# Strassen's seven products in the second dense layer of a fused attention and feed-forward kernel

## The chip, the cores and the metric

The kernel runs on one core of one Trainium2 chip. The metric is the device time of one execution in microseconds (us), the median of several; one execution is taken with the hardware profiler, and its views are what is called "the profile" or "the trace" here. Most times of one kernel agree within about 0.3%.

## The reference

For 8 batches and 12 heads of 448 tokens, attention without softmax, then a two-layer feed-forward on the 3584 tokens:

```python
scores = scale * q @ k.T                      # head_dim 64
attn   = maximum(scores, 0) ** 2 / S
x      = (attn @ v), heads side by side       # 3584 x 768
h      = x @ w_in                             # 768 x 2048
g      = h * sigmoid(1.702 * h)
out    = g @ w_out                            # 2048 x 768, float32
```

## The kernel before

Tokens are worked on in 8 groups of 3 or 4 tiles of 128 (3,4,3,4,3,4,3,4). While the first layer of group g runs on TensorE, the second layer of group g-1 is mixed in, and every 4.8 us of modelled dense time an attention "visit" (three score steps, sometimes one attention-value step) is put between. I call "stage g" the time from the first first-layer matmul of group g to that of group g+1, and "tail" what follows the last first-layer matmul. A "piece" is a run of matmuls that add up in one bank of PSUM, the memory that TensorE writes to. The bank is free for the next piece when another engine has read it out; for the second layer I call that the eviction. All dense pieces, whichever layer, share a pool of two PSUM banks:

```python
ps_s = ctx.enter_context(tc.tile_pool(name="ps_s", bufs=3, space=bass.MemoryType.PSUM))  # 2 banks each
ps_m = ctx.enter_context(tc.tile_pool(name="ps_m", bufs=2, space=bass.MemoryType.PSUM))  # 1 bank each
...
def release():                       # the third score step of a visit is held until now
    while held:
        u, j, sc = held.pop()
        ats[u, j] = relu2(u, j, sc)  # relu on ScalarE, square (at) on VectorE
...
def m1(g, f):                        # first layer, 6 matmuls of 384 or 512 columns
    ht = ps_m.tile([128, 512], F32, name="ht", tag="mm")
    ...                              # gelu on ScalarE empties the bank, GpSimd scales into gt
    release()

def m2(g, m, h):                     # second layer, 16 matmuls of 384 columns
    op = ps_m.tile([128, 512], F32, name="op", tag="mm")
    for f in range(NF):
        nc.tensor.matmul(out=op[:, 0:w], lhsT=gts[g][:, f, m * 128:(m + 1) * 128], rhs=..., ...)
    nc.vector.tensor_scalar(out=ot[:, lo:lo + w], in0=op[:, 0:w], ...)   # eviction on VectorE
    ...
    release()
```

After a visit the inputs of a later unit are prepared: k is cast to float16 on VectorE, q on GpSimd, and both are transposed by DMA.

## Time and profile before

| | before |
|---|---|
| median (lowest to highest) | 403.76 us (403.63 to 404.41), 3 runs |
| span of the profiled run | 402.6 us |
| TensorE / VectorE / ScalarE / GpSimd busy | 95 / 47 / 51 / 33% |
| second-layer matmuls | 912 |
| waits of TensorE after 110 us | none listed |

The page's chain line follows the work that ended last back to the start, and gives each engine's share of the span:

```profile
PE 87%; DVE 5%; ACT 4%; issue 2%; DMA 1%; POOL 0%; ACTq 0%; POOLq 0%
```

TensorE is the bound; the others appear on the chain only in the first quarter. The further lines stand in the prediction.

### The profile page before, as it was taken

The page shows a single profiled execution, that of the slowest core. Times are in us where ns is not written, and L with a number is a line of the kernel's source. Part 1 is how long each engine was busy: PE and PEld are TensorE (multiplying, and loading weights), DVE is VectorE, ACT ScalarE, POOL GpSimd, SP SyncE. Part 2 cuts the span into 40 slices and gives each one's busy share as a digit, 9 for nine tenths or more (in the row PEclk, how much of TensorE's full clock was granted, in tenths as well). Part 3 has the DMA queues.
Part 4 walks back from the last instruction along what each step waited for, and adds up shares of the span by engine and source line. Part 5 has one row for each costly group of instructions (what it writes and reads, how often), then busy time and mean ns, then how long its engine had stood idle before and what let it go on. Part 6 is the DMA issues. An engine that isn't in the chain of part 4 may idle for free.

```text
span 402.6 us, 7803 instructions
## 1 busy us (share of the span) xinstructions
PE 384.2 (95%) x3200; PEld 202.9 (50%) x3200; DVE 187.7 (47%) x296; ACT 204.8 (51%) x295; POOL 133.7 (33%) x200
## 2 busy tenths in 40 slices
PE   7678999999999999999999999999999999999995
PEld 3343545344455555445455555445455555555564
DVE  2886674267655554546446555556444311010121
ACT  3885671576764554665555546566646411322100
POOL 8454425442533223424324232313311222323100
PEclk9989999999999999999999999999999999999999
DMA  8999998988688666573786189915400111111133
GB/s 122 192 205 205 204 277 194 276 147 176 159 181 178 158 126 157 150 145 82 178 157 130 11 192 198 189 22 77 86 16 26 39 41 40 41 39 41 39 80 79
DMA packets 65220, 50.85 MB, mean 126 GB/s; under 512 B 35744, under 2 KB 61728, under 8 KB 65184
## 3 DMA queue, kind: packets, MB, share of 16 engines
q1 hardware_dynamic: 47792, 35.60, 37.2%
q0 software_dynamic: 17152, 14.55, 24.3%
q8 instruction: 25, 0.41, 0.4%
q10 hardware_dynamic: 240, 0.20, 0.2%
q14 instruction: 11, 0.09, 0.1%
HBM read 45.61 MB, written 11.01 MB: 141 GB/s over the span
## 4 chain that ended last, share of the span: by engine, by line
PE 87%; DVE 5%; ACT 4%; issue 2%; DMA 1%; POOL 0%; ACTq 0%; POOLq 0%
PE op L304 36%; PE ht L275 35%; PE sc L141 8%; PE av L166 7%; ACT rl L155 4%; DVE at L156 2%; DMA q<-in_q_dram 1%; DVE qT L131 1%; PE tr L127 1%; DVE rl L152 1%; ACT gf L280 1%; DVE xt L183 0%; DVE kT L131 0%; DVE k L102 0%; POOL k L117 0%
## 5 line engine op out<-in xcount | busy, mean ns | idle before, releaser
L155 ACT ACTIVATE rl<-sc 128x896 f16<-128x896 f32 x165 | 146.0, 920 | 71.7 <-PE sc L141 71.6
L275 PE MATMUL ht<-xt,win 128*128 128x384 f16 (+1 forms) x768 | 157.2, 353 | 1.4 <-DVE xt L183 1.0
L304 PE MATMUL op<-wout,gt 128*128 128x384 f16 (+1 forms) x912 | 153.2, 323 | 0.0
L282 POOL TENSOR_SCALAR gt<-gf 128x384 f16<-128x384 f32 (+1 forms) x128 | 80.1, 626 | 216.5 <-ACT gf L280 215.9
L156 DVE TENSOR_TENSOR at<-rl 128x896 f16<-128x896 f16 x168 | 110.9, 664 | 85.0 <-ACT rl L155 84.7
L280 ACT ACTIVATE gf<-ht 128x384 f32<-128x384 f32 (+1 forms) x128 | 70.3, 549 | 98.4 <-PE ht L275 86.1
L304 PEld LDWEIGHTS <-gt 128*128 128x128 f16 x912 | 88.3, 98 | 60.1 <-issue 1.6
L275 PEld LDWEIGHTS <-win 128*128 128x128 f16 x768 | 71.3, 98 | 77.6 <-issue 16.7
L310 DVE TENSOR_SCALAR osb<-op 128x384 f32<-128x384 f32 (+1 forms) x57 | 31.4, 550 | 115.2 <-PE op L304 115.2
L141 PE MATMUL sc<-qT,kT 64*64 64x448 f16 x672 | 49.3, 366 | 8.7 <-DVE qT L131 3.6
L166 PE MATMUL av<-at,v 64*64 64x448 f16 x672 | 37.8, 359 | 2.0 <-DVE at L156 1.6
L141 PEld LDWEIGHTS <-kT 64*64 64x64 f16 x672 | 18.3, 107 | 35.2 <-issue 22.7
L183 DVE CAST xt<-av 128x768 f16<-128x768 f32 (+2 forms) x36 | 26.8, 772 | 2.5 <-PE av L166 2.5
L166 PEld LDWEIGHTS <-v 64*64 64x64 f16 x672 | 20.2, 109 | 14.3 <-issue 3.9
L89 POOL DMA_DIRECT2D v<-in_v_dram x24 | 17.9, 748 | 16.7 <-PE sc L141 11.0
L102 POOL CAST q<-qst 128x896 f16<-128x896 f32 x18 | 17.3, 964 | 0.2
L102 DVE CAST k<-kst 128x896 f16<-128x896 f32 x18 | 14.8, 821 | 0.0
L131 DVE COPY kT<-tr 128x896 f16<-128x896 f16 x6 | 3.7, 621 | 6.9 <-PE tr L127 6.9
L322 POOL DMA_DIRECT2D win<-in_moe_w_in_dram x8 | 5.4, 682 | 2.3 <-DMA q<-in_q_dram 1.2
L117 POOL DMA_DIRECT2D q<-in_q_dram x6 | 4.3, 719 | 4.1 <-PE sc L141 2.4
L117 POOL DMA_DIRECT2D k<-in_k_dram x6 | 4.5, 757 | 2.2 <-DMA v<-in_v_dram 1.4
L358 PE MATMUL zp<-zero 128*128 128x512 f16 x8 | 3.6, 628 | 1.2 <-DVE zero L355 1.2
(18 smaller groups left out, 27.5 us busy)
## 6 DMA issues: line engine op xcount, KB each, us to landing
out_dram<-osb SPq DMA_DIRECT2D x54, 192.0 KB, 2.7
kst<-in_k_dram SPq DMA_DIRECT2D x18, 448.0 KB, 5.2
qst<-in_q_dram SPq DMA_DIRECT2D x18, 448.0 KB, 5.7
v<-in_v_dram POOLq DMA_DIRECT2D x24, 224.0 KB, 5.1
win<-in_moe_w_in_dram POOLq DMA_DIRECT2D x8, 384.0 KB, 11.5
wout<-in_moe_w_out_dram POOLq DMA_DIRECT2D x4, 768.0 KB, 11.4
k<-in_k_dram POOLq DMA_DIRECT2D x6, 224.0 KB, 9.0
q<-in_q_dram POOLq DMA_DIRECT2D x6, 224.0 KB, 8.8
```

What stands on the lines that cost most here:

```text
L89: nc.gpsimd.dma_start(out=x, in_=quad(v, b, pr))
L102: eng.tensor_copy(out=o, in_=i)
L141: nc.tensor.matmul(out=sc[c, a, 0:S], lhsT=st["kT"][r, j, c], rhs=st["qT"][r, :, c], start=True, stop=True)
L155: nc.scalar.activation(out=rl, in_=sc[:, :, 0:S], func=AF.Relu)
L156: nc.vector.tensor_tensor(out=at, in0=rl, in1=rl, op=ALU.mult)
L166: nc.tensor.matmul(out=st["av"][64 * a:64 * a + 64, s, 0:S], lhsT=st["v16"][r, a, 64 * j:64 * j + 64], rhs=at[r, a, :], start=(j == 0), st ...
L183: nc.vector.tensor_copy(out=xts[g][:, 2 * pr:2 * pr + 2, 64 * (lo - gcum[g]):64 * (hi - gcum[g])], in_=av[:, :, 64 * (lo - b * J):64 * (hi ...
L275: nc.tensor.matmul(out=ht[:, 0:n], lhsT=w[:, kk, fo:fo + 128], rhs=xts[g][:, kk, 0:n], start=(kk == 0), stop=(kk == NK - 1))
L280: nc.scalar.activation(out=gf[:, 0:n], in_=ht[:, 0:n], func=AF.Gelu_apprx_sigmoid, scale=1.0 / SC)
L282: nc.gpsimd.tensor_scalar(out=gts[g][:, f, 0:n], in0=gf[:, 0:n], scalar1=SC, scalar2=1.0, op0=ALU.mult, op1=ALU.mult)
L304: nc.tensor.matmul(out=op[:, 0:w], lhsT=gts[g][:, f, m * 128:(m + 1) * 128], rhs=wout[h][f // WO][:, f % WO, part * w:(part + 1) * w], sta ...
L310: nc.vector.tensor_scalar(out=ot[:, lo:lo + w], in0=op[:, 0:w], scalar1=1.0 / SC, scalar2=None, op0=ALU.mult)
```

## The change

From group 1 on, pairs of tiles are multiplied by Strassen's scheme (halves of d_ff and halves of the output columns): seven products of 8 matmuls instead of eight. To pay for it, sums of activation halves are formed on VectorE, sums of weight halves once on VectorE and GpSimd, and the products are combined in the evictions (ScalarE for the first two, VectorE for the rest) with three additions per pair on GpSimd. An odd tile is done with the same weights at its old matmul count. Some buffers shrink to make room. The core of the diff:

```diff
-    stp = ctx.enter_context(tc.tile_pool(name="stp", bufs=3))
+    stp = ctx.enter_context(tc.tile_pool(name="stp", bufs=2))
-    osp = ctx.enter_context(tc.tile_pool(name="osp", bufs=4))
+    osp = ctx.enter_context(tc.tile_pool(name="osp", bufs=3))
...
+    def pair(g, m, n):
+        A = [[part_of(g, m + i, j) for j in range(2)] for i in range(2)]
+        if n == 0:
+            asum(5, None, A[0][0], A[0][1], ALU.add)
...
+        elif n == 3:
+            asum(1, None, A[0][0], A[1][1], ALU.add)
+        elif n == 4:
+            asum(6, A[1][0], A[1][0], A[0][0], ALU.subtract)
...
+        op = bank()
+        if n == 0:
+            product(A[0][0], w_b, op)
+            evac(ea, op, None)                       # ScalarE
...
+        elif n == 3:
+            product(sums[2], wout[0][0], op)
+            evac(o1[:, lo], op, eb)                  # VectorE
+            nc.gpsimd.tensor_tensor(out=eb, in0=ec, in1=o1[:, lo], op=ALU.subtract)
+        elif n == 4:
+            product(sums[7], w_e, op)
+            evac(o0[:, lo], op, ea)
+        elif n == 5:
+            product(sums[1], w_a, op)
+            evac(o0[:, lo], op, o0[:, lo])
+            evac(o1[:, hi], op, eb)
...
+            c = [("single", g - 1, nm - 1, h) for h in (1, 0)] if nm % 2 else []
+            c += [("pair", g - 1, m, n) for m in range(0, nm - 1, 2) for n in range(7)]
...
+                weight_sum(w_e, wout[0][1], wout[1][1], ALU.add, i, nc.vector)
+                if i == gblk[0] // 2 - 1:
+                    weight_sum(w_e, wout[0][1], wout[1][1], ALU.add, 3, nc.vector)
+                    for i in range(4):
+                        weight_sum(w_d, wout[1][0], wout[0][0], ALU.add, i, nc.gpsimd)
```

More of the change, by code (lines that the diff above doesn't have):

```diff
@@ L55 @@
     gfp = ctx.enter_context(tc.tile_pool(name="gfp", bufs=3))
-    gtp = ctx.enter_context(tc.tile_pool(name="gtp", bufs=2))
-    osp = ctx.enter_context(tc.tile_pool(name="osp", bufs=4))
+    gtp = ctx.enter_context(tc.tile_pool(name="gtp", bufs=1))
+    smp = ctx.enter_context(tc.tile_pool(name="smp", bufs=1))
+    osp = ctx.enter_context(tc.tile_pool(name="osp", bufs=3))
     ps_s = ctx.enter_context(tc.tile_pool(name="ps_s", bufs=3, space=bass.MemoryType.PSUM))
@@ L63 @@
     warm = cst.tile([1, 1], F32, name="warm")
-    zero = cst.tile([128, 512], F16, name="zero")
     win = [cst.tile([128, NK, WQ * 128], F16, name=f"win{i}") for i in range(NF // WQ)]
@@ L67 @@
             for h in range(2)]
+    wsum = [cst.tile([128, WO, NOUT], F16, name=f"wsum{i}") for i in range(3)]
     units = {}
@@ L269, in m1 @@
         if f == 0:
-            gts[g] = gtp.tile([128, NF, 512], F16, name="gt", tag="gt")
+            gts[g] = gtp.tile([128, NF, n], F16, name="gt", tag=f"gt{g % 2}")
         ht = ps_m.tile([128, 512], F32, name="ht", tag="mm")
@@ L298, in m2 @@
         ot = osb[g, m]
-        last = g == NG - 1 and m == gblk[g] // 2 - 1
-        for part in range(2 if last and h == 1 else 1):
-            w = NOUT // 2 if last and h == 1 else NOUT
-            op = ps_m.tile([128, 512], F32, name="op", tag="mm")
-            for f in range(NF):
-                nc.tensor.matmul(
-                    out=op[:, 0:w],
-                    lhsT=gts[g][:, f, m * 128:(m + 1) * 128],
-                    rhs=wout[h][f // WO][:, f % WO, part * w:(part + 1) * w],
-                    start=(f == 0), stop=(f == NF - 1))
-            lo = h * NOUT + part * w
-            nc.vector.tensor_scalar(out=ot[:, lo:lo + w], in0=op[:, 0:w],
-                                    scalar1=1.0 / SC, scalar2=None, op0=ALU.mult)
-            if last:
-                store(g, m, lo, lo + w, (nc.sync, nc.scalar))
@@ L314, in m2 @@
-        if h == 1 and not last:
+        op = ps_m.tile([128, 512], F32, name="op", tag="mm")
+        for f in range(NF):
+            nc.tensor.matmul(
+                out=op[:, 0:NOUT],
+                lhsT=gts[g][:, f, m * 128:(m + 1) * 128],
+                rhs=wout[h][f // WO][:, f % WO, :],
+                start=(f == 0), stop=(f == NF - 1))
+        lo = h * NOUT
+        nc.vector.tensor_scalar(out=ot[:, lo:lo + NOUT], in0=op[:, 0:NOUT],
+                                scalar1=1.0 / SC, scalar2=None, op0=ALU.mult)
@@ new lines, in m2, with weight_sum, part_of, asum @@
+        if h == 1:
+            store(g, m, 0, DM, (nc.sync, nc.sync))
+        release()
+    HF = NF // 2
+    w_a, w_b, w_c = wsum
+    w_d, w_e = wout[1][0], wout[0][1]
+    def weight_sum(o, x, y, op, i, eng):
+        c = slice(2 * i, 2 * i + 2)
+        eng.tensor_tensor(out=o[:, c, :], in0=x[:, c, :], in1=y[:, c, :], op=op)
+    def part_of(g, m, i):
+        return gts[g][:, i * HF:(i + 1) * HF, m * 128:(m + 1) * 128]
+    sums = {}
+    def asum(n, out_, x, y, op):
+        if out_ is None:
+            out_ = smp.tile([128, HF, 128], F16, name=f"as{n}", tag=f"as{n}")
+        nc.vector.tensor_tensor(out=out_, in0=x, in1=y, op=op)
+        sums[n] = out_
@@ new lines, in product, with bank, evac @@
+    def product(lhs, w, op, start=True, stop=True, c0=0, cw=NOUT):
+        for f in range(HF):
+            nc.tensor.matmul(
+                out=op[:, 0:cw], lhsT=lhs[:, f, :], rhs=w[:, f, c0:c0 + cw],
+                start=(start and f == 0), stop=(stop and f == HF - 1))
+    def bank():
+        return ps_m.tile([128, 512], F32, name="op", tag="mm")
+    def evac(o, op, add, w=NOUT):
+        if add is None:
+            nc.scalar.activation(out=o, in_=op[:, 0:w], func=AF.Copy, scale=1.0 / SC)
+        else:
+            nc.vector.scalar_tensor_tensor(out=o, in0=op[:, 0:w], scalar=1.0 / SC, in1=add,
+                                           op0=ALU.mult, op1=ALU.add)
@@ new lines @@
+    et = {}
+    def pair(g, m, n):
+        A = [[part_of(g, m + i, j) for j in range(2)] for i in range(2)]
+        last = g == NG - 1 and m == gblk[g] // 2 - 2
+        if n == 0:
+            asum(5, None, A[0][0], A[0][1], ALU.add)
+            for x in "ab":
+                et[x] = smp.tile([128, NOUT], F32, name=f"e{x}", tag=f"e{x}")
+            for i in range(2):
+                osb[g, m + i] = osp.tile([128, DM], F32, name="osb", tag="osb")
+        elif n == 1:
+            asum(2, None, A[1][0], A[1][1], ALU.add)
+        elif n == 2:
+            asum(7, A[0][1], A[0][1], A[1][1], ALU.subtract)
+        elif n == 3:
+            asum(1, None, A[0][0], A[1][1], ALU.add)
+        elif n == 4:
+            asum(6, A[1][0], A[1][0], A[0][0], ALU.subtract)
+        lo, hi = slice(0, NOUT), slice(NOUT, DM)
+        o0, o1 = osb[g, m], osb[g, m + 1]
+        ea, eb, ec = et["a"], et["b"], o1[:, hi]
+        if n == 6 and last:
+            w = NOUT // 2
+            for p in range(2):
+                op = bank()
+                product(sums[6], w_d, op, c0=p * w, cw=w)
+                c = slice(NOUT + p * w, NOUT + (p + 1) * w)
+                evac(o1[:, c], op, o1[:, c], w)
+                store(g, m + 1, c.start, c.stop, (nc.sync, nc.scalar))
+            return
+        op = bank()
+        if n == 0:
+            product(A[0][0], w_b, op)
+            evac(ea, op, None)
+        elif n == 1:
+            product(A[1][1], w_c, op)
+            evac(eb, op, None)
+            nc.gpsimd.tensor_tensor(out=ec, in0=ea, in1=eb, op=ALU.add)
+        elif n == 2:
+            product(sums[5], wout[1][1], op)
+            evac(o0[:, hi], op, ea)
+            nc.gpsimd.tensor_tensor(out=ea, in0=ec, in1=o0[:, hi], op=ALU.subtract)
+        elif n == 3:
[9 more added lines that the diff above has]
+            evac(o1[:, hi], op, eb)
+            store(g, m, 0, DM, (nc.sync, nc.sync))
+            if last:
+                store(g, m + 1, 0, NOUT, (nc.sync, nc.sync))
+        else:
+            product(sums[6], w_d, op)
+            evac(o1[:, hi], op, o1[:, hi])
+            store(g, m + 1, 0, DM, (nc.sync, nc.sync))
+        release()
@@ new lines, in single @@
+    def single(g, m, h):
+        A = [part_of(g, m, j) for j in range(2)]
+        if h == 1:
+            osb[g, m] = osp.tile([128, DM], F32, name="osb", tag="osb")
+            asum(3, None, A[0], A[1], ALU.add)
+        op = bank()
+        product(A[1 - h], (w_c, w_b)[h], op, stop=False)
+        product(sums[3], wout[h][h], op, start=False)
+        nc.vector.tensor_scalar(out=osb[g, m][:, h * NOUT:(h + 1) * NOUT], in0=op[:, 0:NOUT],
+                                scalar1=1.0 / SC, scalar2=None, op0=ALU.mult)
+        if h == 0:
@@ L353 @@
         nc.scalar.activation(out=warm, in_=warm, func=AF.Gelu_apprx_sigmoid)
-        nc.vector.memset(zero, 0.0)
+        zero = gfp.tile([128, 1024], F16, name="zero", tag="gf")
+        nc.vector.memset(zero[:, 0:512], 0.0)
         zp = ps_m.tile([128, 512], F32, name="zp", tag="mm")
         for _ in range(8):
-            nc.tensor.matmul(out=zp, lhsT=zero[:, 0:128], rhs=zero, start=True, stop=True)
+            nc.tensor.matmul(out=zp, lhsT=zero[:, 0:128], rhs=zero[:, 0:512], start=True, stop=True)
         load16(0, "k")
@@ L441 @@
                 prefetch(9, 8)
+            for i in range(4):
+                o, x, y, op = ((w_b, wout[1][0], wout[1][1], ALU.subtract),
+                               (w_a, wout[0][0], wout[1][1], ALU.add),
+                               (w_c, wout[0][1], wout[0][0], ALU.subtract))[m]
+                weight_sum(o, x, y, op, i, nc.vector)
         def step_visit():
@@ L456 @@
             a = [("m1", g, f) for f in range(NF)] if g < NG else []
-            c = [("m2", g - 1, m, h) for m in range(gblk[g - 1] // 2) for h in range(2)]
+            nm = gblk[g - 1] // 2
+            c = [("single", g - 1, nm - 1, h) for h in (1, 0)] if nm % 2 else []
+            c += [("pair", g - 1, m, n) for m in range(0, nm - 1, 2) for n in range(7)]
             for x in mix(a, c):
@@ L471 @@
                     m1_done = g + 1
-            else:
+            elif it[0] == "m2":
                 m2(*it[1:])
                 acc += T2
+                i = it[2]
+                weight_sum(w_e, wout[0][1], wout[1][1], ALU.add, i, nc.vector)
+                if i == gblk[0] // 2 - 1:
+                    weight_sum(w_e, wout[0][1], wout[1][1], ALU.add, 3, nc.vector)
+                    for i in range(4):
+                        weight_sum(w_d, wout[1][0], wout[0][0], ALU.add, i, nc.gpsimd)
+            elif it[0] == "single":
+                single(*it[1:])
+                acc += T2
+            else:
+                pair(*it[1:])
+                acc += T2 / 2
             while acc >= tv and visits:
```

## The prediction

> **What bounds the kernel now.** I read the page's busy times and slices first, then the costliest groups, then the busy time by stage, and last single pieces of the timeline.
>
> ```profile
> span 402.6 us, 7803 instructions
> ...
> PE 384.2 (95%) x3200; PEld 202.9 (50%) x3200; DVE 187.7 (47%) x296; ACT 204.8 (51%) x295; POOL 133.7 (33%) x200
> ...
> PE   7678999999999999999999999999999999999995
> ...
> DVE  2886674267655554546446555556444311010121
> ```
>
> TensorE is busy in nearly every slice after the start, VectorE never above eight tenths. The groups say what TensorE does, and who serves it:
>
> ```profile
> L156 DVE TENSOR_TENSOR at<-rl 128x896 f16<-128x896 f16 x168 | 110.9, 664 | 85.0 <-ACT rl L155 84.7
> ...
> L304 PE MATMUL op<-wout,gt 128*128 128x384 f16 (+1 forms) x912 | 153.2, 323 | 0.0
> ...
> L310 DVE TENSOR_SCALAR osb<-op 128x384 f32<-128x384 f32 (+1 forms) x57 | 31.4, 550 | 115.2 <-PE op L304 115.2
> ```
>
> The second layer (op, L304) never waits; its eviction by VectorE (L310) always waits for TensorE. VectorE idles 85 us before the squaring (at) because its queue stands still until ScalarE's relu is there. By stage:
>
> ```profile
> core 0: us, PE busy (x) PEld busy (x) DVE busy (x) ACT busy (x) POOL busy (x), PEclk, DMA share, GB/s
> ...
> 160.00:250.00 90.00, 90.00 (x751) 47.08 (x751) 47.38 (x73) 53.50 (x77) 30.60 (x44) 1.00 0.66 140
> 250.00:340.00 90.00, 90.00 (x720) 47.84 (x719) 37.18 (x60) 44.32 (x65) 23.30 (x37) 1.00 0.30 61
> ```
>
> From 110 us on the list of waits has none for TensorE, and the clock is 1.00. So a removed matmul should be worth its whole stream time, provided that nothing makes TensorE wait. Whether it will wait is read from how late the servants come after one attention visit (12 scores into three buffers; two relus at once, the third "held" until the next dense piece is issued):
>
> ```profile
> 184.13 0.76 PE L141 MATMUL sc<-qT,kT 64*64 64x448 f16 x12
> ...
> 184.80 1.72 ACT L155 ACTIVATE rl<-sc 128x896 f16<-128x896 f32 x2
> ...
> 184.83 2.76 PE L275 MATMUL ht<-xt,win 128*128 128x512 f16 x12
> ...
> 185.74 0.62 DVE L156 TENSOR_TENSOR at<-rl 128x896 f16<-128x896 f16 x1 [1.71 <-ACT rl L155]
> ...
> 186.39 0.61 ACT L280 ACTIVATE gf<-ht 128x512 f32<-128x512 f32 x1
> ...
> 186.89 0.93 ACT L155 ACTIVATE rl<-sc 128x896 f16<-128x896 f32 x1
> ...
> 187.78 1.03 DVE L102 CAST k<-kst 128x896 f16<-128x896 f32 x1
> 188.74 1.02 DVE L156 TENSOR_TENSOR at<-rl 128x896 f16<-128x896 f16 x1
> ```
>
> The third relu ends 3.69 us after the visit began (187.82), since it queues behind two relus and a gelu; the squaring that needs it comes after that. Any eviction issued later on VectorE waits behind it. Today this costs nothing, because a second-layer piece runs 2.60 us (16 matmuls) and its PSUM bank is wanted only one more piece later.
>
> **What the Trainium skill says.** "PSUM — Partial Sum Buffer", section "Engine vs sequencer instructions": ScalarE, VectorE and GpSimd queues are strict first in, first out. The trace agrees (the 85 us above). "VectorE: DVE Perf Modes", "Side-by-side: where the cycles go for N=2048 bf16": 16-bit operands go two per cycle, plus a fixed part of about 150 cycles. The squaring agrees: 896/2/0.96 GHz = 467 ns, and the undisturbed ones take 620, so 155 fixed. "GPSIMD Engine Reference", section 3.1: a two-input elementwise op takes about 2.6 cycles per element; this trace has none. "SBUF — State Buffer", "Who interferes with whom": a VectorE op with two SBUF inputs contends with a GpSimd op that reads SBUF. The squaring at 188.74 took 1.02 instead of 0.62 us while GpSimd was at work beside it, which fits.
>
> **The change part by part.** Groups 1 to 7 have 4,3,4,3,4,3,4 tiles: 11 pairs and 3 single tiles. *Removed*: each pair needs 7 products of 8 matmuls instead of 64 matmuls. A matmul of 384 columns costs 2.60/16 = 0.1625 us, so 11 x 8 x 0.1625 = 14.3 us. (912 matmuls become 816: 88 of these 96, and 8 half-width ones that only come from splitting the last piece.) The single tiles save nothing.
>
> *Added on VectorE*: per pair 5 sums of 1024 f16 elements, estimated 1024/2/0.96+155 = 0.69 us, and 6 evictions instead of 4, at 0.56: 3.4+1.1 = 4.6 us, for 11 pairs 50; 3 sums for singles, 2; 16 weight sums of 768 elements at 0.56, 9. Together 61, so VectorE 188 to 249 us. *ScalarE*: 22 evictions at about 0.5, 11 us. *GpSimd*: 33 additions of 384 f32, estimated with the skill's 2.6 cycles at 384x2.6/1.2 GHz = 0.83 plus some 0.15, 33 us; 4 weight sums of 1.8, 7 us. All beside TensorE, and no engine reaches its limit on the average.
>
> The weight sums: 12 lie on VectorE after 65.9 us, where it has 6 us idle before the first squaring at 77.8, so hidden. The four on GpSimd begin as group 1's first layer ends and hold its queue 7 to 9 us; the three gf buffers cover about that. I allow 0.5 us.
>
> *Moved*, the point that I think decides: a piece of 16 matmuls becomes pieces of 8 (1.30 us), while the same two PSUM banks serve first layer and products, and the sum for a later product is issued on VectorE ahead of the eviction of the present one. The instruction order of the changed kernel confirms it: held squaring, sum, eviction. A piece N+2 needs the bank of N, so the eviction of N has only piece N+1 to finish in.
>
> Worked for "visit, first-layer piece, product with a sum, first-layer piece, next" with 384 columns (first layer 6 x 0.1625 = 0.975). TensorE would want the bank at 0.69+0.975+1.30+0.975 = 3.94 us after the visit's start. VectorE: with the shorter gelu the held squaring begins about 3.53, queue steps are 0.54 (squaring) and 0.61 (sum), eviction 0.56, signal 0.05: done at 5.3. Stall 1.35 us. With a visit that also holds an attention-value step (2.0 us long, held squaring at about 4.55): wanted 5.25, done 6.3, stall 1.05. A product directly after the visit: squarings done 2.95, then sum and eviction, 4.17, wanted 2.97: 1.2. Without a sum 0.6. With two evictions (product 6 of 7) 1.05. Products evicted by ScalarE (first two): 0 to 0.1. With a product just before a visit: 0, as attention uses other banks.
>
> Going through the issue order stage by stage (first layer of group g beside second layer of g-1), these cases sum to: stage 2, 4.9 us; 3, 2.0; 4, 3.8; 5, 3.3 (with 1.65 for the single tile, whose sum is needed within its own piece); 6, 3.3. Together 17. The k casts on VectorE (0.6 to 1.0 us each, one every second or third visit) and slower ops beside GpSimd add an estimated 4. Stage 7 and the tail have no attention: VectorE needs 5x0.61+6x0.5 = 6.1 of every 9.1 us, so stalls are only at the double eviction, about 0.1 per pair, and some 0.7 at the very last, where the half products wait for it: 1.
>
> Sum: 403.8 - 14.3 + 17 + 4 + 1 + 0.5 = 412. My hand-worked stalls start every visit from the same lag, and a stalled TensorE lets the others catch up and can spare a later stall, so I take off 3: 409.
>
> **Rivals.** (a) Full gain: the evictions hide as before, 403.8 - 14.3 + 1 = 390.5. For it: no TensorE wait at all after 110 us, VectorE at 53% in 160:250. Against: halved pieces with the same two banks. (b) VectorE as the bound: in stages 2 and 4 per visit period of about 6.2 us it has 1.9 (squarings), 0.9 (casts), 1.4 (sums), 1.1 (evictions) = 5.3, 85%. With a quarter more from contention it would be the limit, and these stages of some 45 us each would stretch by 5 to 10%: 415 to 420. (c) GpSimd holds the chain: its additions stand between evictions of products 3 and 5, but two pieces (2.6 us) lie between against 1 us of work; only with ops of over 2 us does it matter. (d) Stores: with three instead of four output tiles an eviction could wait for a store (2.7 us to landing); I see at least five pieces between, so no effect. One staging buffer less only delays loads that are wanted some 12 us later.
>
> **Range and chances.** The gain is sure to about 0.5 us; the stalls carry the spread: 9 to 28 us. That gives 399 to 418. Over 2% faster needs less than about 6 us of stalls, which I give 0.12; over 2% slower needs over 22, 0.32.
>
> **What would show it.** Right: 816 op matmuls at unchanged spacing, and TensorE waits for PSUM of 15 us or more, put down to VectorE's evictions, between 110 and 340 us; VectorE 240 to 255 us busy; a nearly unbroken stretch after 340 us, shorter by about 4 us. Wrong: TensorE 95% busy again with no such waits (then the bank argument fails), or waits on GpSimd or stores, or sums that take over 1 us.

## More of the kernel before

The experiments ran on two chips: placement alone, the control and the last two kernels on one, the others on another. Each ran beside the kernel before, so the ratios carry the comparison; a difference of medians between two experiments is good to 1 or 2 us.

## The result

The changed kernel takes 420.06 us (419.46 to 421.44, 4 runs), the kernel before 404.08 us beside it. The ratio is 1.0401, 95% interval 1.0372 to 1.0430. A ratio here is the mean of one kernel's fast runs over that of the other's of the same rounds, so it is not quite the ratio of the medians. It is slower by 4%, outside the predicted range by 2 us.

The same parts of the page as before, for the changed kernel:

```profile
span 418.4 us, 7858 instructions
...
PE 377.1 (90%) x3104; PEld 194.8 (47%) x3104; DVE 263.3 (63%) x392; ACT 216.4 (52%) x317; POOL 183.0 (44%) x237
...
PE   7868999899979999899798898799979899999994
...
DVE  2886668576899576465748578745965656222363
...
PE 61%; DVE 18%; ACT 9%; issue 7%; DMA 2%; POOL 0%; SPq 0%; ACTq 0%; DVEq 0%; POOLq 0%
```

The 96 matmuls are gone (3104 instead of 3200), yet TensorE's slices now show eights and sevens up to the last fifth of the span, and the chain runs through VectorE for 18% of it. The list of waits (who waited for whom: us in total, times, longest) names the cause of the holes:

```profile
PE ht L277 <- DVE osb L353: 6.6, 8, 2.4
PE op L342 <- DVE osb L353: 6.4, 7, 1.5
PE op L342 <- ACT gf L282: 3.8, 6, 0.6
...
PE ht L277 <- ACT gf L282: 2.8, 1, 2.8
...
PE op L342 <- DVE as L337: 1.5, 1, 1.5
```

The first two lines are TensorE waiting for an eviction (osb) to empty a bank. The third looks like another matter, ScalarE's gelu, but belongs to it: each of these six products waited for the gelu of the first-layer piece just before it, so it was put in that piece's bank, and in all six places the product in the other bank was still not evicted when TensorE went on (its eviction ended 0.2 to 1.6 us later). With evictions first, below, none of the six waits is left. The busy times by stage, to be held against those in the prediction:

```profile
160.00:250.00 90.00, 82.15 (x659) 41.94 (x658) 55.82 (x83) 51.00 (x75) 35.49 (x48) 1.00 0.61 121
250.00:340.00 90.00, 81.81 (x675) 41.65 (x674) 61.04 (x90) 49.16 (x71) 34.12 (x44) 1.00 0.42 91
```

TensorE falls from 90.00 to 82 of 90 us in both, at full clock, with VectorE at 62 and 68%: busier, but not full. One stall in full, from the timeline (start, duration, engine, and in brackets what the engine had waited for):

```profile
164.33 1.48 PE L342 MATMUL op<-wout,gt 128*128 128x384 f16 x8
...
165.13 2.57 DVE L158 TENSOR_TENSOR at<-rl 128x896 f16<-128x896 f16 x2 [1.34 <-ACT rl L157]
...
165.64 1.46 PE L277 MATMUL ht<-xt,win 128*128 128x512 f16 x6
165.74 0.94 POOL L104 CAST q<-qst 128x896 f16<-128x896 f32 x1
...
167.63 0.61 DVE L104 CAST k<-kst 128x896 f16<-128x896 f32 x1
...
168.16 0.55 DVE L353 SCALAR_TENSOR_TENSOR osb<-op,osb 128x384 f32<-128x384 f32 x1
...
168.76 1.46 PE L277 MATMUL ht<-xt,win 128*128 128x512 f16 x6 [1.66 <-DVE osb L353]
```

The product of 164.33 is done within 1.5 us. Its eviction starts at 168.16, because VectorE takes its queue in order: first two squarings of the visit, one of them slowed by GpSimd's cast of q beside it (2.57 us for two, which take 1.24 undisturbed), then the cast of k, then the eviction. The first-layer piece in the other bank ends in the meantime, and TensorE stands.

Where the 15.8 us between the two profiled spans lie, from the starts of the matmuls in the traces (us):

| | before | changed | difference | matmul time saved there |
|---|---|---|---|---|
| start and stage 0 | | | +0.3 | 0 |
| stage 1 | 41.9 | 42.9 | +1.0 | 0 |
| stage 2 | 46.0 | 51.5 | +5.5 | 2.6 |
| stage 3 | 46.7 | 49.3 | +2.6 | 1.3 |
| stage 4 | 48.1 | 50.9 | +2.9 | 2.6 |
| stage 5 | 45.9 | 49.6 | +3.7 | 1.3 |
| stage 6 | 41.7 | 43.6 | +1.9 | 2.6 |
| stage 7 and tail | 57.1 | 53.8 | -3.3 | 3.9 |
| after the last matmul | | | +1.2 | 0 |

Stages 2 to 6, which have attention, lost 16.6 us although 10.4 us of matmuls had gone: 27.0 us of new loss. Of these the trace counts 21.5 us as idle time of TensorE (none before), and 1.7 us are lost to a stretch of 3.4 us at half clock in stage 2; the other 4 us lie in TensorE's busy time, where the ends of matmuls are modelled, and were not resolved further. Only where there is no attention did the saving arrive.

The largest single event is in stage 2, as four weight sums run on GpSimd:

```profile
112.39 7.43 POOL L327 TENSOR_TENSOR wout<-wout,wout 128x768 f16<-128x768 f16 x4
112.45 2.05 DVE L158 TENSOR_TENSOR at<-rl 128x896 f16<-128x896 f16 x1 [1.50 <-ACT rl L157]
...
114.90 3.43 DVE L327 TENSOR_TENSOR wout<-wout,wout 128x768 f16<-128x768 f16 x2
...
118.25 3.74 DVE L158 TENSOR_TENSOR at<-rl 128x896 f16<-128x896 f16 x2
...
120.40 0.92 ACT L157 ACTIVATE rl<-sc 128x896 f16<-128x896 f32 x1 [2.31 <-DVE at L158]
...
122.90 0.48 ACT L282 ACTIVATE gf<-ht 128x384 f32<-128x384 f32 x1
...
123.43 2.08 PE L277 MATMUL ht<-xt,win 128*128 128x384 f16 x6 [2.80 <-ACT gf L282]
```

Squarings of 0.62 us take 2.05 beside these sums, and two weight sums of VectorE's own take 3.43 us between them. ScalarE's next relu waits for the squarings (its output buffers are full), the gelu queues behind the relu, and TensorE waits 2.80 us. Its first six matmuls afterwards take 2.08 us where the others of this shape take 1.14: the granted clock was 0.89 on the average of 112 to 127 us.

```profile
112.00:127.00 15.00, 12.20 (x81) 6.19 (x79) 14.55 (x13) 8.21 (x13) 13.35 (x12) 0.89 0.73 131
```

In these 15 us VectorE (the third of the busy times) is busy for 14.55, and it stays without a gap until 136 us: here load does bind for a while. In no 15 us clear of this stretch, after stage 0, is it busy for more than about 90%, and over whole stages its share is 79% in stage 2 and at most 73% in the others.

### The profile page after: what moved, and what is told of

It is laid out like the page before. It is cut to its first block, busy times and chain, and to the rows that moved or that the text cites. A ratio compares the mean times of both kernels' runs of the same rounds, so it can differ in the third digit from the quotient of the medians.

```text
span 418.4 us, 7858 instructions
## 1 busy us (share of the span) xinstructions
PE 377.1 (90%) x3104; PEld 194.8 (47%) x3104; DVE 263.3 (63%) x392; ACT 216.4 (52%) x317; POOL 183.0 (44%) x237
## 3 DMA queue, kind: packets, MB, share of 16 engines
q0 software_dynamic: 17152, 14.55, 23.6%
## 4 chain that ended last, share of the span: by engine, by line
PE 61%; DVE 18%; ACT 9%; issue 7%; DMA 2%; POOL 0%; SPq 0%; ACTq 0%; DVEq 0%; POOLq 0%
PE ht L277 26%; PE op L342 21%; ACT rl L157 8%; DVE at L158 7%; PE sc L143 6%; PE av L168 5%; DVE osb L353 3%; PE op L303 2%; DVE k L104 2%; ACT gf L282 2%; DMA kT<-k 1%; DVE wsum L327 1%; DVE xt L185 1%; PE tr L129 1%; DVE as L337 1%
## 5 line engine op out<-in xcount | busy, mean ns | idle before, releaser
L158 DVE TENSOR_TENSOR at<-rl 128x896 f16<-128x896 f16 x168 | 125.8, 756 | 84.3 <-ACT rl L157 83.9
L342 PEld LDWEIGHTS <-gt 128*128 128x128 f16 x408 | 39.1, 98 | 35.2 <-issue 9.5
L342 PE MATMUL op<-wout,as 128*128 128x384 f16 x224 | 41.2, 329 | 4.6 <-DVE osb L353 1.7
L342 PEld LDWEIGHTS <-as 128*128 128x128 f16 x312 | 30.3, 98 | 30.8 <-issue 9.2
L342 PE MATMUL op<-wsum,gt 128*128 128x384 f16 x224 | 40.7, 326 | 0.0
L342 PE MATMUL op<-wout,gt 128*128 128x384 f16 (+1 forms) x184 | 32.4, 319 | 5.3 <-DVE osb L353 3.8
L337 DVE TENSOR_TENSOR as<-gt 128x1024 f16<-128x1024 f16 x36 | 28.4, 799 | 0.0
L353 DVE SCALAR_TENSOR_TENSOR osb<-op,osb 128x384 f32<-128x384 f32 (+1 forms) x23 | 12.3, 536 | 19.3 <-PE op L342 19.2
L398 POOL TENSOR_TENSOR ea<-osb 128x384 f32<-128x384 f32 x11 | 13.3, 1206 | 17.1 <-DVE osb L353 17.1
L342 PE MATMUL op<-wsum,as 128*128 128x384 f16 x88 | 16.1, 326 | 2.2 <-ACT gf L282 1.3
```

The costliest lines, as they stand in the source:

```text
L158: nc.vector.tensor_tensor(out=at, in0=rl, in1=rl, op=ALU.mult)
L337: nc.vector.tensor_tensor(out=out_, in0=x, in1=y, op=op)
L342: nc.tensor.matmul(out=op[:, 0:cw], lhsT=lhs[:, f, :], rhs=w[:, f, c0:c0 + cw], start=(start and f == 0), stop=(stop and f == HF - 1))
L353: nc.vector.scalar_tensor_tensor(out=o, in0=op[:, 0:w], scalar=1.0 / SC, in1=add, op0=ALU.mult, op1=ALU.add)
```

## The experiments

Two theories stood against each other. *Lag*: a product of 8 matmuls leaves its bank's eviction only one short piece of time, and the eviction comes late because it is queued behind less urgent work; the order is at fault. *Load*: VectorE and GpSimd have too much to do (sums, additions, contention); the work is at fault. All results are correct except where said. Lateness below is counted from a trace: for each wait of TensorE for a bank, the time from when the eviction could have started to when it did, by what its engine did in it.

### One part alone: the weight sums off GpSimd

```diff
-                    for i in range(4):
-                        weight_sum(w_d, wout[1][0], wout[0][0], ALU.add, i, nc.gpsimd)
+            for i in {("pair", 1, 0, 0): (0,), ("pair", 1, 0, 2): (1,), ("m1", 2, 6): (2, 3)}.get(it, ()):
+                weight_sum(w_d, wout[1][0], wout[0][0], ALU.add, i, nc.vector)
```

> The changed kernel, with the four sums for the last summed weight moved from GpSimd, where they ran back to back for 7.4 us at the start of stage 2, to VectorE, one or two at a time ahead of an attention visit. Theory: they blocked VectorE's two-input squarings (2.05 us each beside them), hence ScalarE's relus and gelu, hence TensorE for 3.0 us, and the clock fell to half for some 14 matmuls afterwards (another 2 us); so 4 to 6 us of the span come back (414 to 416 us), all of it in stage 2, and no clock dip is left at 123 us. Rival: the stall is part of a lag that the visits cause anyway and only moves: under 2 us gained (over 418 us).

Measured: 416.64 us, ratio to before 1.0340 (1.0292 to 1.0388). VectorE's timeline in the same place, with the last two sums of the weight before it on VectorE:

```profile
116.34 1.02 DVE L327 TENSOR_TENSOR wout<-wout,wout 128x768 f16<-128x768 f16 x2
117.28 1.30 DVE L158 TENSOR_TENSOR at<-rl 128x896 f16<-128x896 f16 x2
```

The same two sums that took 3.43 us now take 1.02, and the squarings after them are undisturbed. Stage 2 shrinks by 4.7 us (51.5 to 46.8), and the 2.80 us wait is gone from the list. In stage 3 this trace loses 1.3 us again: a wait of 2.35 us, which the changed kernel has too, is here followed by 3.4 us at half clock. The profiled execution was the slowest of four, and it began stage 1 2.3 us later; the medians give 3.4 us, a little less than the 4 to 6 expected. So the blockade was real and its own loss: 3.4 us by the medians, 4.7 us in its stage, of which 1.7 are the half clock that followed it.

### One part alone: the sums after the evictions

```diff
         elif n == 3:
-            asum(1, None, A[0][0], A[1][1], ALU.add)       # ahead of the product
...
             evac(o1[:, lo], op, eb)
+            asum(1, None, A[0][0], A[1][1], ALU.add)       # products 2, 3, 4 alike
```

> The changed kernel, with the sums that belong to products 2, 3 and 4 issued on VectorE after the eviction of that product instead of before it. Theory of the prediction (a bank is released by the end of a chain held squaring, sum, eviction, and each link counts): about twelve stalls get shorter by the 0.6 us of a sum, so 5 to 8 us faster than the changed kernel (412 to 415 us), with perhaps 0.1 us given back per pair in the tail. Rival (casts and port contention set the lag, the order of sum and eviction does not): under 3 us (over 417 us).

Measured: 417.78 us, ratio 1.0363 (1.0328 to 1.0397). A gain of 2.3 us in the medians, where 5 to 8 were expected: a miss, inside the bound that the rival had set (under 3), and as the intervals of the two ratios overlap, hardly clear of noise. The squaring and the casts in front of the evictions stayed, and the list of waits for osb still has 13.5 us (13.0 before).

### The kernel before, in halves

```diff
-            c = [("m2", g - 1, m, h) for m in range(gblk[g - 1] // 2) for h in range(2)]
+            c = [("half", g - 1, m, h, q) for m in range(gblk[g - 1] // 2) for h in range(2) for q in range(2)]
+    def m2half(g, m, h, q):          # 8 matmuls, own bank, own eviction; the second adds to the first
```

> The kernel before, with every second-layer piece of groups 1 to 7 cut into two accumulations of 8 matmuls, each with its own PSUM bank and eviction (the second adds to the first). Same matmuls, no sums, no weight sums, nothing on GpSimd; only the piece length of the change. Theory (short pieces on two banks let the lag behind visits through): TensorE waits of 6 to 12 us appear, 410 to 416 us. Rival (short pieces are harmless and the added sums, additions and contention make the whole loss): 404 to 406 us.

Measured: 420.39 us, ratio 1.0419 (1.0395 to 1.0443). The waits:

```profile
PE op L305 <- DVE osb L315: 6.8, 10, 1.8
PE op L305 <- DVE osb L312: 5.2, 9, 1.1
```

This kernel has no Strassen sums, no weight sums, no additions on GpSimd, and VectorE at 51%. Cutting the pieces alone costs 16.7 us, more than the 6 to 12 that I expected and as much as the whole change lost. In its trace the evictions before the waits were late by 12.8 us behind squarings and 5.1 us behind casts of k (a recount of the same trace gives 12.7 and 6.8). The load of the sums cannot explain that. What this run does add for VectorE is 24 us of further evictions (212.0 us busy instead of 187.7); whether they or the order are at fault is settled below, by the same kernel with another order.

### The changed kernel without its sums

```diff
-        nc.vector.tensor_tensor(out=out_, in0=x, in1=y, op=op)
-        sums[n] = out_
+        sums[n] = x
```

> The changed kernel without the sums of activation tiles on VectorE (products take one of the two terms as it is; the result is wrong on purpose, the matmuls and evictions are the same). It takes 42 us of VectorE's work and 58 links from the chains. Theory of the prediction: stalls with a sum in their chain lose 0.6 us or more each and the single tiles' 1.7 us goes, so 10 to 14 us faster than the changed kernel: 406 to 410 us. Rival (VectorE has room, the loss is from short pieces, casts and the weight sums on GpSimd): less than 6 us, over 414 us.

Measured: 413.80 us, ratio 1.0241 (1.0208 to 1.0275); its result is wrong by design. With 43 us less VectorE work (263.3 to 220.3) it gains 6.3 us, between the two expectations. Ten microseconds of loss remain beside 14.3 of matmuls removed. The sums matter, and are the smaller part. This run takes away their load and their places in the queue together, so it does not part the two.

### Only the order: evictions first

```diff
     def release():
         while held:
             u, j, sc = held.pop()
-            ats[u, j] = relu2(u, j, sc)
+            rl = ...; nc.scalar.activation(out=rl, in_=sc[:, :, 0:S], func=AF.Relu)
+            later.append(lambda: square(u, j, rl))       # squaring: later
...
-                cast(prepped[0], "k", nc.vector); cast(prepped[0], "q", nc.gpsimd); trans(prepped[0])
+                later.append(prep)                       # casts and transposes: later
...
+            if it[0] != "m1":
+                flush()                                  # "later" = after the eviction of a second-layer piece
+    # also ahead of the next visit, and ahead of the second of two first-layer pieces; sums after evictions
```

> The changed kernel with nothing taken away: only the order on VectorE (and of the preparation of the next unit) differs. From stage 2 on the squaring of the held score, the casts and transposes of the next unit and the sums are issued after the eviction of the following product instead of before it. Theory (the lag of the eviction behind work that is not urgent, on two banks, is the loss): of the evictions' lateness in the changed kernel (9.0 us behind squarings, 4.6 behind casts, 3.9 behind sums) most goes; 8 to 14 us faster than 420, so 406 to 412; the stall behind GpSimd's weight sums in stage 2 stays. Rival (VectorE and GpSimd are simply too loaded, or contend, in these stages): under 4 us faster, over 416.

Measured: 409.66 us, ratio 1.0155 (1.0132 to 1.0178). Nothing was taken away: VectorE is busy for 265.6 us, 2.3 more than in the changed kernel. Yet 10.4 us return, as the theory of lag had it. The waits that are left:

```profile
PE op L360 <- DVE osb L371: 7.5, 10, 1.9
...
PE ht L295 <- ACT gf L300: 2.8, 1, 2.8
PE ht L295 <- DVE osb L371: 1.9, 2, 1.1
```

The six waits for a gelu and the one for a sum are gone, and TensorE's idle time in stages 2 to 6 falls from 21.5 to 13.0 us. The gf wait of 2.8 us is that of the weight sums, which this edit leaves. I had expected most of the lateness behind squarings to go too; it did not (a recount gives 11.9 us, in the changed kernel 10.7). What went is that behind sums and most of that behind casts. The squarings that remain ahead are those that a visit issues at once.

### The halves again, evictions first

The same edit on the kernel in halves (without sums, as it has none).

> The kernel before in halves (420.4 us), with the same reordering: evictions ahead of held squarings and casts. Theory: the 16 us that the short pieces cost are VectorE lag (12.8 us of squarings and 5.1 of casts ahead of the evictions), so they go nearly all: 405 to 409 us. Rival (short pieces cost of themselves, by restarting TensorE's stream or by ScalarE's lag): over 414 us.

Measured: 409.87 us, ratio 1.0158 (1.0134 to 1.0182), just above the expected range: 10.5 of the 16.7 us return. The waits show it:

```profile
PE op L323 <- DVE osb L333: 2.7, 7, 0.8
...
PE op L323 <- DVE osb L330: 1.0, 2, 0.5
```

12.0 us of waits have become 3.7, with VectorE's work unchanged (212.1 us). What remains is mostly eviction behind the two squarings that a visit issues at once, which this edit does not move. Of the 6.2 us that the cut still costs, 2.5 are in no listed wait.

### Both: evictions first, weight sums off GpSimd

> Both: evictions first and the four weight sums off GpSimd. If the two losses are separate, they add: 3 to 5 us below the run with evictions first alone, 402 to 408 us. If the weight sums' stall was only part of the same lag: no further gain.

Measured: 405.65 us, ratio 1.0065 (1.0039 to 1.0091), 4.0 us below evictions first alone, as the same edit gained 3.4 us in the changed kernel. (Evictions first alone had no half clock in stage 2; there the edit takes 3.2 us off the stage.) The two losses are separate and add.

### And visits only ahead of a first-layer piece

```diff
-            while acc >= tv and visits:
+            nxt = moe[n + 1][0][0] if n + 1 < len(moe) else "m1"
+            while acc >= tv and visits and (tv < 4 or nxt == "m1"):
```

> As the last, and attention visits are put only where the next dense piece is a first-layer piece (its bank is emptied by ScalarE), never right before a product. The stall that then remains in theory is the double eviction of product 6 of 7 (0.3 us each) and late gelus: 394 to 402 us, below the kernel before. Rival (delayed visits pile up and are forced at the group's end): no better than the last, over 404 us.

Measured: 401.55 us, ratio 0.9946 (0.9923 to 0.9969): below the kernel before. No product now directly follows a visit (12 did from stage 2 on), so that its eviction does not meet the visit's own squarings: the waits for osb with a product next fall from 8.0 to 2.9 us.

### Placement alone

The last edit on the changed kernel, with everything else as it was.

> The changed kernel with only the placement of attention visits altered (a visit only where a first-layer piece follows); evictions stay behind squarings, casts and sums, and GpSimd keeps its weight sums. Theory of the prediction: the stalls of products issued right after a visit (1.05 to 1.2 us each, about eight of them) go, those of product after visit and first-layer piece stay or grow: 3 to 7 us faster than the changed kernel, 413 to 417 us, clearly less than evictions first (409.7). Rival (placement was the main fault): under 408 us.

Measured: 414.52 us, ratio 1.0259 (1.0234 to 1.0284): 5.5 us gained in the medians, as expected. Placement alone leaves evictions late behind held squarings, casts and sums, and more of its waits are for a gelu (8 of 0.6 us instead of 6).

### Control: the kernel before, evictions first

> Control: the kernel before (whole pieces of 16 matmuls) with evictions ahead of held squarings and casts. Theory: its evictions are late too, but 2.60 us pieces hide that, so nothing is gained: 403 to 405 us. Rival (the reordering is good in itself, whatever the piece length, and the gains of the runs before are owed to that): 400 us or less.

Measured: 404.38 us beside 404.39, ratio 0.9996 (0.9977 to 1.0016). With pieces of 16 matmuls the order on VectorE makes no measurable difference. It is the short pieces that made it matter.

### Two more moves, for a better version

```diff
         for m in range(gblk[0] // 2):
             m2(0, m, 0)
             if m == 0:
                 prefetch(9, 8)
+        for m in range(3):
             for i in range(4):
                 o, x, y, op = ((w_b, wout[1][0], wout[1][1], ALU.subtract),
...
+        tail = g == NG - 1           # in the tail the sums stay ahead of the evictions
```

> The reordered and re-placed kernel (401.6 us), with two more moves of VectorE work: the 12 weight sums after the three first evictions instead of between them, and in the tail, where no first-layer piece lies between products, the sums ahead of the evictions again. Theory: 1.1 us of TensorE wait in stage 1 and 0.7 us in the tail go: 399 to 400.5 us. Rival: the sums then delay the first squarings of stage 1 and nothing is gained.

Measured: 399.79 us, 6 runs, ratio 0.9893 (0.9874 to 0.9913), the fastest of all kernels here. What its list has left of waits for VectorE in the dense layers after stage 1:

```profile
PE op L360 <- DVE osb L371: 3.0, 6, 1.2
...
PE op L360 <- DVE as L355: 1.2, 2, 1.0
...
PE ht L295 <- DVE osb L371: 0.8, 1, 0.8
```

Stages 1 to 7 with the tail take 320.9 us against 327.2 before. Of the 6.4 us, 1.5 are lost again after the last eviction: 5.3 us to the end of the span instead of 3.8, as six stores are issued one after another in the last 4 us.

### The cast of q on VectorE

```diff
-                    cast(u, "q", nc.gpsimd)
+                    cast(u, "q", nc.vector)
```

> The last, with the cast of q moved from GpSimd (0.94 us, beside which a squaring on VectorE takes up to 2.1 us) to VectorE (estimated 0.62 us, as the undisturbed k cast). Theory (port contention with the cast makes the remaining late evictions): 1 to 3 us faster. Rival (VectorE at 65% has no room, an op more in its queue costs as much as the contention): no change or 1 us slower.

Measured: 400.88 us, 6 runs, ratio 0.9934 (0.9911 to 0.9956): no gain, as the rival had it. The squarings do get faster (89.1 us in all from stage 1 on, instead of 95.9), but the evictions that TensorE waits for now stand behind casts of q: by the recount they are late by 2.6 us behind squarings and 2.8 behind casts of q, where it was 4.7 and none.

## Why the prediction was wrong

The steps that explain the direction held: short pieces on two banks let VectorE's lag through. What failed is the size of terms in the sum: the stalls, for which 17 + 4 - 3 = 18 us were put down and 22 to 24 measured, and the weight sums on GpSimd, 0.5 us put down and 3.4 to 4.7 measured. The sum came out too small, and the range with it.

- *Removed work*: right. 816 second-layer matmuls remain at the old spacing, and where nothing disturbs (stage 7 and tail) the 3.9 us arrive, less 0.6.
- *Short pieces on two banks*: right in kind, and shown three times: the cut alone costs 16.7 us in the kernel before; the order alone returns 10.4 us in the changed kernel; the same order does nothing to long pieces. The worked stalls plus casts and contention (17 + 4) stand against 27.0 us measured in stages 2 to 6, of which 3.4 belong to the weight sums. That leaves 23.6 for 21 (22.3, if the 4.7 us of their stage are taken). By stage, with the 4.7 us off stage 2, the loss is 3.4, 3.9, 5.5, 5.0 and 4.5 us, where the hand-worked stalls, without casts and contention, gave 4.9, 2.0, 3.8, 3.3 and 3.3. The split inside was less good: I took the sum in the chain for the main link, and moving it gained 2.3 us where I expected 5 to 8, while casts of k, put down as an extra, were ahead of the late evictions for 4.6 us.
- *"The four on GpSimd ... I allow 0.5 us"*: the step that failed first. I checked only whether the three gf buffers cover GpSimd's absence, and not what 7.4 us of GpSimd reads do to VectorE's squarings. They made relu, gelu and TensorE wait; 3.4 us by the medians, 4.7 in the stage.
- *"VectorE 240 to 255 us busy"*: failed, it is 263.3. The added work was sized right (61 put down, 60.7 without the squarings); the excess is the squarings, 125.8 us instead of 110.9, slowed beside GpSimd's work.
- *"so I take off 3"*: failed. Nothing in the profile supported this allowance, and the measured stalls, larger than the sum before it was taken off, show no sign of it.
- *"12 lie on VectorE ... so hidden"*: failed by 1.0 us in stage 1. They were hidden from attention, but stood ahead of the evictions of three consecutive second-layer pieces. Moving them gave the time back.
- *The end*: not foreseen, 1.2 us more between last eviction and end; I had estimated the tail's standstill (1, measured 0.6) and left the stores out.
- *"The trace agrees (the 85 us above)"*: misread. At none of the longer waits for a relu in the kernel before did a finished product stand behind the squaring, so they do not show that VectorE's queue is in order. The changed kernel does: at 194.46 us a squaring has waited 1.2 us for its relu, while a product that was done at 194.22 is evicted only at 195.60, after it.

The account closes, the stalls being what the other terms leave: the missing 10.6 us (15.8 in the profiled spans against 5.2 predicted) are 3.0 for the allowance, 2.9 for the weight sums, 2.6 for the stalls, 1.0 for stage 1 and 1.5 for start and end, less 0.4 for the tail. With the weight sums at 4.7 us, 1.3 move from the stalls to them.

- *Rival (a)*, full gain: refuted. *Rival (b)*, VectorE as the bound, 415 to 420: its number fits (420.06), but its cause is refuted by evictions first, which gains 10.4 us with slightly more VectorE work; only for some 23 us of stage 2, beside and after the weight sums, was VectorE full. *Rivals (c) and (d)*, GpSimd's additions and stores on the path: GpSimd and the stores' queue have 0% of the chain, and TensorE's list has no wait for either.

Open: of the 14.3 us, the best version has 4.6. About 5 us of waits are counted in its trace, mostly an eviction behind two squarings of a visit, and 1.5 us are lost at the end; some 3 us are not accounted for. Whether a third bank would end the waits I could not try, as attention holds the other six.

## What to carry to other kernels

Halving a piece of work on the busiest engine halves the time in which its buffer must be emptied, so before counting the matmuls saved, look at how late the emptying engine's queue gets after its worst burst, and count everything issued ahead of it. If it is late, look at the order in which that engine's work is issued before its amount: emptying first, then what nobody waits for. Here the order was worth 10.4 us, and leaving out the sums 6.3. Side work "on an idle engine" is only free if it does not slow one that is needed.

## What the Trainium skill lacked or had wrong

- "SBUF — State Buffer", "Who interferes with whom", says that a VectorE op with two SBUF inputs contends with a GpSimd op that reads SBUF, without a duration for such a pair. Here a float16 squaring of 0.62 us took 2.05 beside back-to-back float16 sums on GpSimd and, in all runs together, 1.13 on average beside one cast from float32 to float16 (72 cases). The section also says that issue order, not the shape of the op, decides who blocks, and the traces agree: beside one float32 addition the squaring took 0.61 to 0.63 us where the addition began after it (49 cases), and 0.72 to 1.42 where the addition began before it (40 cases).
- "TensorE: Matmul & The Clock Gate", "Why this matters for your kernels", warns of idle gaps of more than about 3 us. Here shorter gaps were followed by 3.4 us at half clock, though not each time: four of five listed gaps of 2.8 us (not the one below, of evictions first), two of three of 2.35 us, and neither of the two of 1.9 us. So the gap that can cost begins below 3 us, and its length alone does not decide.

```profile
122.86 1.14 PE L295 MATMUL ht<-xt,win 128*128 128x384 f16 x6 [2.81 <-ACT gf L300]
```

- No page has the cost of shorter accumulation pieces on a fixed number of PSUM banks. Here, two halves instead of one piece of 16 matmuls cost 16.7 us of 404, and 6.2 with evictions issued first.
